# A four-layer kernel on one core: new token orders for the first convolution, moved product buffers, moved spectrum stores, and the last block's products in rows 1, 3, 5, 7

## The chip, the core and the metric

The kernel runs on one core of a Trainium2 chip. The metric is the device time of one execution in microseconds. A core has a matrix engine (PE; PEld is its weight load), a vector engine (DVE), a scalar engine (ACT), a general engine (POOL), and SP, whose queue issues nearly all DMAs here. Each engine runs its own instructions in order, and engines wait for each other through semaphores. Matmuls write PSUM, and ACT or DVE must copy ("evacuate") the result to SBUF.

## The reference

Four layers over x of shape 2048 x 512: local attention, long convolution, and both again with the same weights. Every layer works on a layer norm of x and adds its result to x.

```
def _A_ref(x, wqkv, wo):                 # 32 heads of 16
    q, k, v = split(x @ wqkv)
    idx = pos[:, None] - 2 * arange(8)   # 8 keys, every second position back
    attn = softmax(where(idx >= 0, q . k[idx] / 4, -1e9))
    return (attn . v[idx]) @ wo
def _B_ref(u, ...):                      # per channel
    K = real(sum_n Cc * exp(dt * A * l) * dt * Bc)
    return irfft(rfft(u, 2L) * rfft(K, 2L))[:L] + u * Dskip
x = x + _A_ref(ln(x)); x = x + _B_ref(ln(x))
x = x + _A_ref(ln(x)); x = x + _B_ref(ln(x))
```

## The kernel before

**Stages.** `k_gen` computes the convolution kernel K in tables (tiles A_t and A_t2 in two table pools, power table pow_t, B_t) and, beside it, the first layer's norm, keys and queries. At its end the first three products of the first attention are formed in tiles A_pr, which lie in the first table pool. Then come attention 0 (`LayerA.core`), convolution 0 (`FftB`, tag 0), attention 1 and convolution 1. All engines but POOL follow an order written out by hand.

**Attention** (`core`, line 307). Queries and keys are worked in 4 blocks (q) of 512 positions and 4 feature tiles (ft). `mult(q, ft)` (289) is one DVE instruction that multiplies a query tile with 8 shifted key tiles into a product tile of the pool `self.prp` (two buffers, 8 KB per partition each). `lsum` (298) sums the products over each head by 32 matmuls into the logits L. `mx` (360), `sub_exp` (366), `recip` (376) and `norm_p` (389) are the softmax. The loop at line 465 does blocks 0 to 2, with the value projections `v_proj` (346) and query projections between. The last value projections start a DMA that copies v one partition on (354, 355); without it no row but the first two can be worked.

The value phase is the loop at line 492 over 16 rows. `pv_mult` (397) is a DVE instruction of the same size (attention times values), `pv_sum` (405) sums it by 32 matmuls, `out_proj` (416) projects the row before and adds x. In between stand the products and the sums of block 3, its query projections and its softmax (max in row 8, reciprocal in row 10, normalisation in row 11):

```
q_proj(3, 0)
q_proj(3, 1)
...
if n in (1, 2, 4, 6):
    mult(3, n // 2)
...
if n in (2, 4):
    q_proj(3, n // 2 + 1)
```

**Convolution** (`FftB`, line 694). It has two groups of 256 channels. Its order is a string of tokens; the last letter says which engine evacuates (A: ACT, D: DVE).

- `K` and `U` (`f1`, 735): first transform of the convolution kernel and of the input, 16 tokens each, 8 for each group.
- `k` (`k_f2`, 754) and `u` (`u_f2`, 797): second transform; it needs all eight first ones of its group. u is always evacuated by ACT.
- `m` (`u_mult`, 786): the product of both spectra, two DVE instructions. Besides the spectrum tile kn it needs a copy ks with partitions exchanged pairwise, which two DMAs make (`kf_load`, 772).
- `y` (`i1`, 805): first inverse transform. `z` (`i2`, 821): second inverse transform and addition to x, with 8 matmuls for D and 12 for A.

All these share four PSUM tiles, so a token's matmuls wait until the fourth token before it is evacuated. Spectrum tiles come from a list `free`, taken from the front; `m` puts both tiles back at the end. `pump` (767) starts the exchange DMAs, at most `ahead` (4) spectra past the multiply. `k_f2` also stores the spectrum to kf_dram, from which convolution 1 reads it. The list `late` holds the last norm pieces of attention 0 (rows 8 to 15), one of which is done after each K token from the second on; U needs them all.

`ORDER0` covers convolution 0 up to half of the y tokens. `ORDERF` has the rest and, between, the front of attention 1: half statistics h, aggregation a, root p, norm n, transposes T with their evacuations E, and key and query projections P and Q.

Of the kernel before, what the change touches and what calls it, by code (L numbers as in the profile page):

```python
# [14 lines left out]
F32 = mybir.dt.float32  # L15
BF16 = mybir.dt.bfloat16
# [4 lines left out]
P = 128  # L21
S = 2048
# [15 lines left out]
NG = 2  # L38
DQG = 64
EC = 16  # L40
NEC = 128 // EC
# [6 lines left out]
zktkKkUEETkeUUktKTkkUkKTUUeKkkpkxpKUxkpUEUxUKkqUxUUUUpqoUkpoxKXUQxoUkpkKXZpxXxpxZZ  # L48
"""
ORDER0 = """  # L50
KA KD KA KD KA KA KD KA KD KA KD kA KD KA KA kD kA kD kA UA KD UA UA UD UA kD UA
UA UD KA UA kD u kD m u u u kA m UA m UD UA u kA m kD u UA u m UA m
UD m UA kA u kD kD u kA u m m kA m u u yD yA m u u m u m yA u yA
yA m m yA m yA yD
"""
ORDERF = """
yA yA yA yA yA yA z00D yA h00 yA z01D h01 z10A z11A h10 a0 p0 h11
n0 z12A z02A a1 z03A h12 S T0 h02 p1 E00A n1 E01A a2 z13A P00 h13 Q00
h03 T1 E10A p2 E11D P01 a3 P02 P03 P10 p3 P11 n2 n3 P12 T2 E20D E21A
P13 T3 E30A P20 P21 x1 P22 P23 E31D  # L60
"""
ORDER1 = """
UD UA UA UD UA UA UD UA UD UA UD u UD u m UA u u m UA m u u UA m UD m
# [52 lines left out]
def rstd_act(nc, pool, var):  # L116
    rstd = pool.tile(list(var.shape), F32, name="ln_rstd")
    nc.scalar.activation(rstd[:], var, ACT.Ln, bias=EPS)
    nc.scalar.activation(rstd[:], rstd[:], ACT.Exp, scale=-0.5)
    return rstd  # L120
# [42 lines left out]
class LayerA:  # L163
# [143 lines left out]
    def core(self, x_sb, u, lnp, ev=None, nprod=0):  # L307

        tc, nc, lnst, l = self.tc, self.nc, self.lnst, self.layer
# [11 lines left out]

        with ExitStack() as c2:
            big = c2.enter_context(tc.tile_pool(name=f"a{l}_big", bufs=1, reuse_waits="tile"))
            self.prp = c2.enter_context(tc.tile_pool(name=f"a{l}_prod", bufs=2, reuse_waits="tile"))
            v = big.tile([P, NA + 14, D], BF16, name="v_ext")
            if self.wv is None:
                self.load_wv(big)
# [1 line left out]
            if l:  # L329
                self.load_wo(big)  # L330
            wk = c2.enter_context(tc.tile_pool(name=f"a{l}_wk", bufs=2, reuse_waits="tile"))
            pavp = c2.enter_context(tc.tile_pool(name=f"a{l}_pav", bufs=2, reuse_waits="tile"))
            ps_q = c2.enter_context(tc.tile_pool(name=f"a{l}_ps_q", bufs=2, space=PSUM))
            ps_o = c2.enter_context(tc.tile_pool(name=f"a{l}_ps_o", bufs=2, space=PSUM))
# [60 lines left out]
            pvs, oTs, lns = {}, {}, {}  # L395
# [35 lines left out]
            def x_stats(a):  # L431
                row_stats(nc, lnst, x_sb[:, a, :], a, "dve")

            def u_begin(a0, a1, eng, rs="pool"):
                lns[a0] = ln_begin(nc, lnp, lnst, a0, a1, eng, rs)

            def u_end(a0):
                lns[a0] = ln_end(nc, lnp, lns[a0])

            def u_apply(a0, rows, eng=None):  # L440
                rstd, nb = lns[a0]
                for a in rows:
                    ln_apply(nc, u[:, :, a, :], x_sb[:, a, :].rearrange("p (q r) -> p q r", r=4), rstd, nb, a - a0,
                             eng or ("dve" if a % 2 else "act"))
# [42 lines left out]
            proj(100)  # L487
            linit(3)
            q_proj(3, 0)
            q_proj(3, 1)  # L490
            rows = [0, 2, 1, *range(3, NA)]
            for n in range(16):
                pv_mult(rows[n])
                if n in (0, 8):
                    mx(2 + n // 8)
                if n in (2, 10):
                    recip(2 + n // 8)
                if n in (4, 11):
                    norm_p(2 + n // 8)
                if n in (1, 2, 4, 6):  # L500
                    mult(3, n // 2)
                if n in (7, 11, 15):
                    u_begin(n - 7, n - 3, "act", "act" if n > 7 else "pool")
                if n in (8, 12):
                    u_end(n - 8)
                if n in (9, 10, 13, 14):
                    b0 = 0 if n < 11 else 4
                    r0 = b0 + (0 if n in (9, 13) else 2)
                    u_apply(b0, range(r0, r0 + 2))
                if n == 15:  # L510
# [12 lines left out]
                if n > 0:  # L523
                    out_proj(rows[n - 1])
                if n in (1, 2, 4, 6):
                    lsum(3, n // 2)
                event(("o", n))
            if l == 0:
                out_proj(15)
                return [lambda: [u_end(8), u_apply(8, range(8, 12), "pool")], lambda: x_stats(14), lambda: x_stats(15),  # L530
                        lambda: u_begin(12, 16, "dve", "act"), lambda: [u_end(12), u_apply(12, range(12, 16), "pool")]]
            u_begin(12, 15, "dve", "act")
            out_proj(15)
            pw = pq_tile()
# [159 lines left out]
class FftB:  # L694
# [566 lines left out]
def kernel(  # L1261
# [16 lines left out]
    nc = tc.nc  # L1278
# [18 lines left out]
    u = xnT[:].rearrange("p t (b r) -> p (t b) r", r=64).rearrange("p q (a r) -> p q a r", r=4)  # L1297
# [38 lines left out]
    with tc.tile_pool(name="ctmp_g2", bufs=1) as g2tmp, tc.manual_schedule(engines=MAN):  # L1336
# [9 lines left out]
    late.append(C["masks"])  # L1346
    krctx2.close()
    la.close_logits()

# [3 lines left out]
    fb.ahead = 4  # L1353
    fb.open_mid()
    with tc.manual_schedule(engines=MAN):
        fb.run(ORDER0, u, k=kp, late=late)
    fb.c_mid.close()
    la.close()
    la = LayerA(tc, nc, consts, lnst, A_wqkv, A_wo, 1, xnT, 1)
# [95 lines left out]
```

## Time and profile before

| What | us |
|---|---|
| median of 8 runs | 431.95 (430.49 to 433.6) |
| the profiled execution, its own time | 433.6 |
| its span, first to last instruction | 431.8 |
| stage: convolution kernel, keys and queries of layer 1 | 0 to about 112 |
| stage: attention 0, logits, then value rows | 112 to 141, 141 to 199.5 |
| stage: convolution 0 | 199.5 to 264.8 |
| stage: front and logits of attention 1 | 264.8 to 322 |
| stage: value rows of attention 1 | 322 to 378 |
| stage: convolution 1 | 380 to 431.8 |

Times inside the span are counted from its start. A bracket at the end of a timeline line is the idle time of the engine just before the instruction, and what ended it. In a group such as "x32" the first time is the start of the first. The costliest waits of PE, ACT and DVE that concern the stages above, from the table of waits, are these: PE's weight load for pav 8.3 us in 12 waits, DVE's cast for PE 7.3 us in 8, DVE's addition to x for PE 7.5 us in 5.

### The profile page before, as it was taken

How to read it: one execution, taken by the hardware profiler on the slowest of the kernel's cores; microseconds unless marked ns; L12 is line 12 of the kernel's file. 1: busy time of each engine (PE TensorE's matmuls, PEld its weight loads, DVE VectorE, ACT ScalarE, POOL GpSimd, SP SyncE). 2: the span in 40 equal slices, each digit the busy share in tenths (PEclk: the TensorE clock that was granted, in tenths of full speed). 3: DMA queues.
4: the chain of work that ended last, by engine and by line, in shares of the span. 5: the costliest groups of instructions: out<-in, count | busy, mean ns of one | idle time of the engine just before them, and what ended most of it. 6: DMA issues, size and time to landing. Idle time of an engine off the chain costs nothing.

```text
span 431.8 us, 12729 instructions
## 1 busy us (share of the span) xinstructions
PE 352.8 (82%) x5502; PEld 264.2 (61%) x5502; DVE 391.9 (91%) x534; ACT 325.8 (75%) x557; POOL 39.1 (9%) x46
## 2 busy tenths in 40 slices
PE   3000259899999989999888999999998999997894
PEld 2000127667655668676877897555566778776794
DVE  8999999999899999995899959879999999889874
ACT  6999999986355488986899998855556469689961
POOL 3000300000692000002200000000000020000000
PEclk9999999999999999999899999999999899999999
DMA  8930832141116742742355670810141085125415
GB/s 221 384 101 12 85 73 70 32 76 48 29 37 186 241 124 89 265 200 101 110 212 216 252 197 24 260 60 2 32 112 30 2 318 188 51 83 168 128 34 164
DMA packets 62466, 54.16 MB, mean 125 GB/s; under 512 B 33893, under 2 KB 50890, under 8 KB 61130
## 3 DMA queue, kind: packets, MB, share of 16 engines
q1 hardware_dynamic: 62266, 53.22, 40.2%
q8 instruction: 43, 0.70, 0.7%
q10 hardware_dynamic: 144, 0.13, 0.1%
q14 instruction: 13, 0.11, 0.1%
HBM read 30.28 MB, written 13.24 MB: 101 GB/s over the span
## 4 chain that ended last, share of the span: by engine, by line
PE 51%; ACT 12%; DVE 12%; DMA 5%; issue 3%; SPq 2%; ACTq 0%; DVEq 0%
PE po L410 9%; PE pk L1150 5%; DVE prod L295 5%; PE pq L349 4%; PE pq L422 4%; ACT a1s L733 4%; PE pp L1088 4%; PE L L302 3%; PE pp L242 3%; DVE pav L402 3%; ACT ub L803 3%; PE pq L185 3%; DMA v_ext<-v_ext 3%; PE pb L816 3%; PE pb L817 2%
## 5 line engine op out<-in xcount | busy, mean ns | idle before, releaser
L402 DVE TENSOR_TENSOR pav<-attn,v_ext 128x4096 bf16<-128x4096 bf16 x32 | 72.8, 2284 | 0.7 <-PE po L410 0.2
L295 DVE TENSOR_TENSOR prod<-qT,kT_ext 128x4096 bf16<-128x4096 bf16 x29 | 66.1, 2298 | 2.2 <-PE L L302 2.1
L410 PEld LDWEIGHTS <-pav 128*128 128x128 bf16 x1024 | 59.2, 98 | 12.2 <-DVE pav L402 8.3
L410 PE MATMUL po<-ident,pav 128*128 128x128 bf16 x1024 | 63.1, 220 | 4.1 <-DVE pav L402 4.0
L1078 PE MATMUL pt<-ident,x_blk 128*128 128x128 bf16 x64 | 6.3, 241 | 43.4 <-ACT x_blk L158 43.4
L990 DVE TENSOR_TENSOR A_t<-A_t,pow_t 128x1024 bf16<-128x1024 bf16 (+4 forms) x46 | 38.3, 872 | 0.2
L351 ACT CAST v_ext<-pq 128x512 bf16<-128x512 f32 x32 | 18.7, 586 | 21.1 <-PE pq L349 19.9
L803 ACT CAST ub<-pb 128x1024 bf16<-128x1024 f32 x32 | 33.0, 1089 | 1.4 <-DVE t L791 1.3
L422 PE MATMUL pq<-wop,oT 128*128 128x512 bf16 x128 | 33.7, 387 | 0.0
L302 PEld LDWEIGHTS <-prod 128*128 128x128 bf16 x928 | 26.8, 96 | 10.3 <-DVE prod L295 5.4
L1078 PEld LDWEIGHTS <-x_blk 128*128 128x128 bf16 x64 | 4.8, 107 | 45.8 <-ACT x_blk L158 44.4
L751 PE MATMUL pb<-a1s,w_sb 128*128 128x64 bf16 x768 | 27.6, 194 | 5.8 <-ACT ub L803 3.3
L816 PE MATMUL pb<-Wp,t 128*128 128x128 bf16 x256 | 30.1, 219 | 1.8 <-ACT ub L803 1.4
L1088 PE MATMUL pp<-xnT,kT_ext 128*128 128x512 bf16 x96 | 26.2, 400 | 6.1 <-ACT qT L1093 3.2
L733 ACT CAST a1s<-pb 128x1024 bf16<-128x1024 f32 x30 | 29.4, 1076 | 1.8 <-PE pb L744 1.7
L349 PE MATMUL pq<-wv,xnT 128*128 128x512 bf16 x128 | 30.7, 379 | 0.0
L413 ACT CAST oT<-po 128x512 bf16<-128x512 f32 x32 | 18.5, 579 | 15.6 <-PE po L410 15.6
L751 PEld LDWEIGHTS <-w_sb 128*128 128x128 bf16 x768 | 25.1, 98 | 8.3 <-issue 7.1
L817 PE MATMUL pb<-WpJ,t 128*128 128x128 bf16 x256 | 30.1, 219 | 0.0
L302 PE MATMUL L<-ind,prod 128*128 128x8 bf16 x928 | 27.5, 166 | 1.8 <-DVE prod L295 1.6
L733 DVE CAST a1s<-pb 128x1024 bf16<-128x1024 f32 x18 | 21.7, 1222 | 7.5 <-PE pb L744 7.3
L817 PEld LDWEIGHTS <-t 128*128 128x128 bf16 x256 | 25.0, 98 | 2.6 <-issue 1.5
(226 smaller groups left out, 855.5 us busy)
## 6 DMA issues: line engine op xcount, KB each, us to landing
w_sb<-w_dram SPq DMA_DIRECT2D x8, 1024.0 KB, 7.8
w_dram<-w_zero SPq DMA_DIRECT2D x1, 4096.0 KB, 14.5
kf_ring<-kf_dram SPq DMA_DIRECT2D x13, 256.0 KB, 3.6
kf_ring<-kf_dram SPq DMA_DIRECT2D x26, 128.0 KB, 3.6
v_ext<-v_ext SPq DMA_DIRECT2D x4, 784.0 KB, 6.1
x_blk<-in_A_x_dram SPq DMA_DIRECT2D x4, 512.0 KB, 4.1
kT_ext<-in_A_wqkv_dram SPq DMA_DIRECT2D x4, 512.0 KB, 9.8
x_sb<-in_A_x_dram SPq DMA_DIRECT2D x4, 512.0 KB, 5.1
```

Of the source, the lines that this page charges most:

```text
L295: nc.vector.tensor_tensor(pr, self.qT[q][:, ft].unsqueeze(1).to_broadcast([P, W, 4, P]), kap, ALU.mult)
L302: self.nc.tensor.matmul(L[:, al, w, ft * 8:(ft + 1) * 8], lhsT=pr[:, w, al, :], rhs=self.c["ind8"][:], start=(ft == 0 and w == 0 and al % ...
L349: nc.tensor.matmul(pp[:], lhsT=xnT[:, dt, a * P:(a + 1) * P], rhs=wv[:, dt, :], start=(dt == 0), stop=(dt == NDT - 1))
L402: nc.vector.tensor_tensor(pv[:], attn[:, n % 4].unsqueeze(2).to_broadcast([P, W, DH, H]), vap, ALU.mult)
L410: nc.tensor.matmul(po[:, ft, :], lhsT=pvf[:, w, ft * P:(ft + 1) * P], rhs=ident[:], start=(w == 0 and ft == 0), stop=(w == W - 1), skip_gr ...
L422: nc.tensor.matmul(pw[:], lhsT=oT[:, ftp, :], rhs=self.wo[:, ftp, :], start=False, stop=(ftp == NDT - 1))
L733: (self.nc.scalar.copy if eng == "act" else self.nc.vector.tensor_copy)(dst, src)
L751: nc.tensor.matmul(p2[:, j, :], lhsT=self.w2[:, ec * EC + j, :], rhs=a1s[:, ec * EC + j, :], start=True, stop=True)
L803: nc.scalar.copy(ub[:], p2)
L816: nc.tensor.matmul(p3[:, j, :], lhsT=t1[:, dql, :], rhs=wp_r, start=True, stop=False)
L817: nc.tensor.matmul(p3[:, j, :], lhsT=t2[:, dql, :], rhs=wpj_r, start=False, stop=True)
L1088: nc.tensor.matmul(pps[kind, b, ft][:], lhsT=la.wqk[:, dt, c:c + P], rhs=la.xnT[:, dt, b * 512:(b + 1) * 512], start=(dt == 0), stop=(dt = ...
```

## The change

1. The product pool is opened after the pool wk instead of before it; in attention 0 a 2 KB tile named gap is put between.
2. In the value phase block 3's products are formed, and summed, in rows 1, 3, 5, 7 instead of 1, 2, 4, 6. Of its query projections only the first is left before the rows; the other three are in rows 1, 3, 5.
3. `ORDER0` and `ORDERF` are replaced. ORDER0 now ends after three y tokens instead of eight, and ORDERF has thirteen. ACT evacuates 10 k, 10 U, 7 K and 13 y (before 8, 12, 9 and 14); DVE 6, 5, 9 and 3 (before 8, 4, 7, 2). One z is on DVE instead of two, four E instead of three. The new string has 15 U tokens where the old one has 16: the first transform of the last 32 channels of group 1 is left out, and the second transform reads what that part of its tile holds.
4. The late pieces are named and ordered by a string; aggregation (g) and root (r) are two pieces instead of one, so there are seven with the masks instead of six. The masks' instructions are POOL's, and in the profile they run at 44 us.
5. The store of the spectrum moves from behind `k_f2` to behind the multiply of the same spectrum. `pump` may now also start an exchange, in convolution 0, whenever more tiles are free than spectra are still to come.

```diff
 ORDER0 = """
-KA KD KA KD KA KA KD KA KD KA KD kA KD KA KA kD kA kD kA UA KD UA UA UD UA kD UA
-UA UD KA UA kD u kD m u u u kA m UA m UD UA u kA m kD u UA u m UA m
-UD m UA kA u kD kD u kA u m m kA m u u yD yA m u u m u m yA u yA
-yA m m yA m yA yD
+KD KA KA KD KA KA KD KA KD KA KD kA kA KD kA KD UA UD UA UD UA kD UA UD UA KD
+kA kD u kD kA u UA m KD m u u UA UA UA m UD u m KA UD u m u kA kD m kA UA
+kD u kA m kA kD u m u kA m m u u yD yA u m yA u m m m u u m m
 """
+LATE0 = "a s t g r b m"
 ORDERF = """
-yA yA yA yA yA yA z00D yA h00 yA z01D h01 z10A z11A h10 a0 p0 h11
-n0 z12A z02A a1 z03A h12 S T0 h02 p1 E00A n1 E01A a2 z13A P00 h13 Q00
-h03 T1 E10A p2 E11D P01 a3 P02 P03 P10 p3 P11 n2 n3 P12 T2 E20D E21A
-P13 T3 E30A P20 P21 x1 P22 P23 E31D
+yA yA yA yA yA yA yD yA yA yA z01D yD yA yA z00A z10A z11A h01 h00 h10 a0 z12A
+p0 h11 z02A n0 a1 z03A h02 S T0 p1 E01D n1 E00A h12 a2 z13A P02 P01 h03 T1
+E10A Q00 E11D p2 P03 P00 n2 h13 P10 P12 a3 T2 E21D E20A p3 n3 P11 P13 P23 P21
+T3 E31D x1 E30A P20 P22
 """
...
-            self.prp = c2.enter_context(tc.tile_pool(name=f"a{l}_prod", bufs=2, reuse_waits="tile"))
...
             wk = c2.enter_context(tc.tile_pool(name=f"a{l}_wk", bufs=2, reuse_waits="tile"))
+            if l == 0:
+                wk.tile([P, 1024], BF16, name="gap", bufs=1)
+            self.prp = c2.enter_context(tc.tile_pool(name=f"a{l}_prod", bufs=2, reuse_waits="tile"))
...
+            def u_aggr(a0, a1):
+                ag = lnp.tile([P, a1 - a0, 2], F32, name="ln_ag")
+                for a in range(a0, a1):
+                    nc.vector.bn_aggr(ag[:, a - a0, :], lnst["bn"][:, a, 0, :])
+                lns[a0] = ag
+            def u_rstd(a0):
+                ag = lns[a0]
+                lns[a0] = rstd_act(nc, lnp, ag[:, :, 1]), ag[:, :, 0], -1.0
...
-            q_proj(3, 1)
...
-                if n in (1, 2, 4, 6):
+                if n in (1, 3, 5, 7):
                     mult(3, n // 2)
...
-                if n in (2, 4):
+                if n in (1, 3, 5):
                     q_proj(3, n // 2 + 1)
...
         self.nk += 1
         self.pump()
-        self.nc.sync.dma_start(self.kf_dram[g, ec].rearrange("p r q e -> (p r) (q e)"), kf.rearrange("p q e -> p (q e)"))
...
+    def room(self):
+        return self.tag == 0 and len(self.free) > NG * NEC - self.nk
     def pump(self):
-        while self.nkf < min(self.nk, self.nm + self.ahead):
+        while self.nkf < self.nk and (self.nkf < self.nm + self.ahead or self.room()):
             self.kf_load(self.nkf)
...
         self.nm += 1
         if self.tag == 0:
+            self.nc.sync.dma_start(self.kf_dram[g, ec].rearrange("p r q e -> (p r) (q e)"), kn.rearrange("p q e -> p (q e)"))
             self.free += [kn, ks]
```

More of the change, by code (lines that the diff above doesn't have):

```diff
@@ L50 @@
 ORDER0 = """
-KA KD KA KD KA KA KD KA KD KA KD kA KD KA KA kD kA kD kA UA KD UA UA UD UA kD UA
-UA UD KA UA kD u kD m u u u kA m UA m UD UA u kA m kD u UA u m UA m
-UD m UA kA u kD kD u kA u m m kA m u u yD yA m u u m u m yA u yA
-yA m m yA m yA yD
+KD KA KA KD KA KA KD KA KD KA KD kA kA KD kA KD UA UD UA UD UA kD UA UD UA KD
+kA kD u kD kA u UA m KD m u u UD UA UA UA m UD u m KA UD u m u kA kD m kA UA
+kD u kA m kA kD u m u kA m m u u yD yA u m yA u m m m u u m m
 """
+LATE0 = "a s t g r b m"
 ORDERF = """
-yA yA yA yA yA yA z00D yA h00 yA z01D h01 z10A z11A h10 a0 p0 h11
-n0 z12A z02A a1 z03A h12 S T0 h02 p1 E00A n1 E01A a2 z13A P00 h13 Q00
-h03 T1 E10A p2 E11D P01 a3 P02 P03 P10 p3 P11 n2 n3 P12 T2 E20D E21A
-P13 T3 E30A P20 P21 x1 P22 P23 E31D
+yA yA yA yA yA yA yD yA yA yA z01D yD yA yA z00A z10A z11A h01 h00 h10 a0 z12A
+p0 h11 z02A n0 a1 z03A h02 S T0 p1 E01D n1 E00A h12 a2 z13A P02 P01 h03 T1
+E10A Q00 E11D p2 P03 P00 n2 h13 P10 P12 a3 T2 E21D E20A p3 n3 P11 P13 P23 P21
+T3 E31D x1 E30A P20 P22
 """
@@ L524, in core @@
                     out_proj(rows[n - 1])
-                if n in (1, 2, 4, 6):
+                if n in (1, 3, 5, 7):
                     lsum(3, n // 2)
@@ L529, in core @@
                 out_proj(15)
-                return [lambda: [u_end(8), u_apply(8, range(8, 12), "pool")], lambda: x_stats(14), lambda: x_stats(15),
-                        lambda: u_begin(12, 16, "dve", "act"), lambda: [u_end(12), u_apply(12, range(12, 16), "pool")]]
+                return {"a": lambda: [u_end(8), u_apply(8, range(8, 12), "pool")], "s": lambda: x_stats(14), "t": lambda: x_stats(15),
+                        "g": lambda: u_aggr(12, 16), "r": lambda: u_rstd(12),
+                        "b": lambda: [u_end(12), u_apply(12, range(12, 16), "pool")]}
             u_begin(12, 15, "dve", "act")
@@ L1345 @@
         late = la.core(x_sb, u, lnp, ev, 3)
-    late.append(C["masks"])
+    late["m"] = C["masks"]
     krctx2.close()
@@ L1355 @@
     with tc.manual_schedule(engines=MAN):
-        fb.run(ORDER0, u, k=kp, late=late)
+        late["."] = lambda: None
+        fb.run(ORDER0, u, k=kp, late=[late[c] for c in LATE0.split()])
     fb.c_mid.close()
```

## The prediction

> **What bounds the kernel now.** I read the page's engine shares first, then the busy time by stage (windows), then the timelines of single engines at the places the diff touches, and last the DMA queue.
>
> ```profile
> PE 352.8 (82%) x5502; PEld 264.2 (61%) x5502; DVE 391.9 (91%) x534; ACT 325.8 (75%) x557; POOL 39.1 (9%) x46
> 141.00:178.00 37.00, 34.64 (x515) 26.26 (x513) 36.59 (x30) 28.17 (x56) 1.02 (x1) 1.00 0.54 154
> 199.50:264.80 65.30, 58.48 (x1357) 54.70 (x1357) 54.92 (x87) 59.83 (x68) 6.37 (x9) 0.97 0.51 176
> 268.30:320.50 52.20, 52.15 (x616) 30.19 (x615) 45.73 (x63) 32.42 (x58) 0.00 (x0) 1.00 0.29 89
> 340.00:378.00 38.00, 37.91 (x517) 29.76 (x516) 35.04 (x42) 26.82 (x66) 2.89 (x1) 1.00 0.45 162
> ```
>
> The columns after the length are busy PE, PEld, DVE, ACT and POOL. DVE's 91% is an average over stages with different limits. In the first attention's value phase (141 to 178 us) DVE is full. In the first convolution (199.5 to 264.8) nobody is: ACT 59.8 and PE 58.5 of 65.3. In the second attention's front and logits, and again from 340 to 378, PE is full. So the same edit is worth something in one layer and nothing in another.
>
> Four places show waits that the diff could touch (timelines of DVE, PE and ACT):
>
> ```profile
> 112.15 0.44 DVE L255 COPY kT_ext<-kT_ext 128x508 bf16<-128x508 bf16 x1
> 114.66 4.49 DVE L295 TENSOR_TENSOR prod<-qT,kT_ext 128x4096 bf16<-128x4096 bf16 x2 [2.08 <-PE L L302]
> ```
> ```profile
> 113.68 0.94 PE L302 MATMUL L<-ind,A_pr 128*128 128x8 bf16 x32
> ...
> 117.01 0.95 PE L302 MATMUL L<-ind,prod 128*128 128x8 bf16 x32 [0.64 <-DVE prod L295]
> ```
> ```profile
> 204.54 0.20 ACT L118 ACTIVATE ln_rstd<-ln_ag 128x4 f32<-128x4 f32 x1 [1.50 <-DVE ln_ag L128]
> ...
> 213.78 7.47 ACT L733 CAST a1s<-pb 128x1024 bf16<-128x1024 f32 x8
> ```
> ```profile
> 255.53 1.23 DVE L836 TENSOR_TENSOR x_sb<-pb,x_sb 128x1024 bf16<-128x1024 f32 x1 [5.01 <-PE pb L833]
> ```
> ```profile
> 334.62 2.54 PE L410 MATMUL po<-ident,pav 128*128 128x128 bf16 x32 [1.25 <-DVE pav L402]
> ```
> ```profile
> kf_dram<-kn SPq DMA_DIRECT2D x7, 256.0 KB, 3.4
> DMA to landing us min/median/max: 2.3/3.2/4.6
> ```
>
> The first pair is the important one: DVE stops for 2.08 us until PE has read A_pr. The product doesn't need A_pr; only its memory does. The last fence is the landing of the spectrum stores (line 761), which the change moves.
>
> **What the Trainium skill says.** Perfetto Trace Analysis, Optimization Strategy: a kernel can have several regimes; look for gaps on the engine that limits each one and for the semaphore behind them. The trace agrees (windows above). DMA: Bandwidth & Descriptors, Two DMAs through the same engine are not ordered: only the completion semaphore orders, so a buffer that a store still reads can't be rewritten before the store has landed; here 2.3 to 4.6 us. SBUF — State Buffer, Who interferes with whom: a DVE instruction with two SBUF inputs contends with a GpSimd one that reads SBUF. The trace agrees in part: at 129.19 us, beside POOL, a product takes 2.70 us against 2.28, but the two from 114.66 are not slowed. TensorE: Matmul & The Clock Gate, What's actually happening: the PE clock halves for windows of 3.4 us after slack. The trace has such windows from 206.1 and from 335.81, each 3.41 us; the second follows the 1.25 us gap above.
>
> **The change part by part.**
>
> *Product buffers (first attention).* Sizes per partition: the products begin 74 KB or so above the constants (residual 16.8, small tiles 0.3, spectrum 16, g2 scratch 8, v and wo 34), i.e. 75 KB to 91 KB. The tables of the kernel generation lie at 64 to 80 (A_t) and 80 to 88 (A_t2), and hold A_pr. That is the overlap behind the 2.08 us. Behind the wk pool (11 KB) and the gap (2 KB) the products begin at 88 KB, past A_t2, over the second table pair, whose last reader (pk, line 1150) ends at 111.1, before DVE is ready at 112.6. So the stall goes. What is late next: the max (line 363) of this block needs the row sums on PE. PE: 4 value projections and two row sums from 111.96 end at 116.2; row sum 0.8 and mask 0.5 bring 117.6, where DVE would stand at 117.05. So DVE keeps 2.08 - 0.55 = 1.5 us. PE's waits for prod (0.79, 0.58, 0.24, 0.36 and 0.30 up to 141) add to 2.2, so PE can follow. DVE is full from there to 183.6, hence **-1.5** at 199.5. Bounds: -2.1 (no wait at the max) and -0.8 (POOL beside DVE costs 0.4 a product twice). The copy of v by DMA (issue 141.15, landing 147.9, needed 148.87) is moved with the projection that starts it and keeps its 1 us.
>
> *Products in rows 1, 3, 5, 7, projections in 1, 3, 5.* Nothing is added; four products of 2.2 us and three projections of 0.86 move. First attention: DVE-bound, the sum before row 8 is the same, 0. The row sum of the last product now comes in row 7; row 8's max needs it at 173.65 and PE has it at 172.95. Second attention: PE idles 0.17 + 0.15 + 1.25 = 1.57 before row 4. Now the projection no longer stands before row 2, which waits for the v copy (326.88): PE idles 1.03 there, and 0.1 later: -0.5. But the max of block 3 now waits for PE: 352.7 instead of 351.36; 13.4 us later (chain to pav of row 12) DVE comes about 0.5 late for PE. I take **-0.2**; bounds -0.5 and +0.3. The half-clock window costs 3.41/2 = 1.7 us; the profiled execution (433.6, span 431.8 and 1.8 around it) pays it, and 433.6 - 1.7 is the median 431.95. So I sum against the median and count no gain there.
>
> *ORDER0, ORDERF, late list.* Counting tokens with the measured spacing (ACT 0.905, DVE cast 1.14, multiply pair 1.2): ACT up to the last i2 58.8 before, 57.0 after; DVE 45.5 and 46.6. One U token fewer (0.44 PE, 0.9 ACT) is in it. ACT ran without a gap from 213.8 to 258. More to the point is the prefix: at the last multiply ACT had 45.3 and DVE 42.0; now 40.7 and 43.1. Splitting aggregation and root saves ACT the 1.50 wait. POOL's second apply (3.0 us) starts at 205.6 instead of 205.28; the first U comes at 209.6, later. Walking: first u evacuated at 217.8, DVE then full to the last multiply at 246.15 (before 249.0). PE is without a gap from y3: 13 y at 0.92, one i2 at 0.88, six at 1.31 = 20.7 from 241.9, i.e. 262.65 against 264.84: **-2.2**. DVE's start of the tail moves from 255.5 to 252.2, which covers one more cast, one more transpose copy (0.6) and a 1.4 wait for z00's ACT copy; the last norm ends 0.9 earlier, so PE's projections stay gapless.
>
> *Moved store.* 16 stores at 0.55 issue each go from behind the spectrum to behind its multiply; the SP queue issues the same 26 us. Behind a waiting swap stand all later swaps and stores. New wait: swap 4 takes kn0, free at multiply 0 (220.15); store 1 is issued by 221.9; swap 6 takes kn1 and waits for it, 221.9 + L; two issues 1.1 and store 3's 0.6; kD9 takes kn3, free at 223.6 + 2L, and is due on DVE at 228.4. Stall = 2L - 4.8, with 0.35 slack. With L = 3.2 (median): 1.6, net **+1.25**. Bounds: L = 2.3 gives 0, L = 4.6 gives +4.05. Queued behind kD9 on DVE: the multiplies 5 to 15, and for them all of y8 to z13. The later group-1 swaps are issued at once (free buffers outnumber what is left), which takes the 0.26 wait of multiply 12; already in the walk.
>
> Sum: -1.5 - 0.2 - 2.2 + 1.25 = -2.65; 431.95 - 2.65 = **429.3** (the profiled kind of execution: 433.6 - 2.65 = 430.95, or 429.25 without the half clock).
>
> **The rivals.**
> All of it (20%): stores land within 2.6, the max doesn't wait: -2.1 - 0.2 - 2.2 = -4.5, 427.45. For: 2.2 to 2.5 is what swaps and kf_nat stores take. Against: the SP queue is near full there.
> Only the memory wait (18%): the convolution's balance brings nothing, as DVE is now filled to 100% and any lag of 1.1 reaches y8: -1.5, 430.45. For: DVE's idle was its slack. Against: ACT had 2.7 idle too.
> It doesn't do what it says (7%): the moved buffers still meet live memory (the gap is 2 KB, my sum of sizes is good to some 0.3 KB), and the 2.08 stays: -1.2, 430.75.
> Slower (13%): the store-before-reuse chain at kD9. The total is 2L - 9.05; it decides from L = 4.5 on, the upper end of what stores showed (4.6). With L = 5.2, +1.35, 433.3. For: v_ext copies took 6.1. Against: stores no longer alternate with the swaps early on.
>
> **How the numbers follow.** Forecast 42% at 429.3 (428.2 to 430.4 alone), the others as given. 0.3% is 1.3 us, what a measurement of this kernel can tell from no change: faster is under 430.65, slower over 433.25. Faster: 42 + 20 + 10 of the 18 = 72; slower: 11 of the slow case's 13; the rest 17. Range: 426.8 to 431.6 leaves out the slow case and a little of the fastest.
>
> **What would show it.** The 2.08 before the first prod gone and the value phase's end 1.5 earlier; z03's last matmul some 1 us earlier relative to the convolution's start; a DVE wait of 1 to 2 us before the tenth k cast put down to a DMA; in the second attention PE idle near row 2 and no 1.25. Wrong if the wait before prod stays, if the k casts wait 4 us or more, or if PE has gaps between y3 and z13.

## The result and the profile after

| What | before | after |
|---|---|---|
| median, us | 432.01 (32 runs) | 428.43 (11 runs) |
| lowest to highest, us | 430.49 to 435.29 | 428.15 to 428.70 |
| profiled execution, its own time, us | 433.6 | 428.58 |
| its span, us | 431.8 | 426.8 |

The ratio is 0.9913, with a 95% interval of 0.9896 to 0.9929: 3.6 us less. The forecast was 429.3 with a range of 426.8 to 431.6. The spread (highest less lowest) fell too, from 4.8 us to 0.55.

One correction comes first. The copy of the new `ORDER0` above lacks a token: its second line reads `... m KD m u u UD UA UA UA m UD ...`. So there are sixteen U tokens, ACT evacuates ten and DVE six of them, and nothing is left out of the computation. Point 3 of the change and the "one U token fewer" of the prediction are my misreading.

The busy shares of the changed kernel (page), and busy time by stage (windows: length, then PE, PEld, DVE, ACT, POOL, granted clock, DMA share, GB/s). The stretches follow the same work as those shown of before:

```profile
PE 354.2 (83%) x5506; PEld 264.3 (62%) x5506; DVE 394.7 (92%) x537; ACT 323.2 (76%) x554; POOL 43.9 (10%) x46
```
```profile
141.00:178.00 37.00, 35.87 (x505) 27.57 (x503) 36.66 (x29) 28.22 (x56) 1.02 (x1) 0.95 0.53 149
198.90:264.10 65.20, 61.29 (x1389) 56.03 (x1388) 58.65 (x99) 60.74 (x70) 6.37 (x9) 1.00 0.52 176
264.10:315.20 51.10, 51.05 (x585) 29.36 (x583) 45.69 (x69) 31.53 (x57) 0.00 (x0) 1.00 0.30 91
337.00:373.00 36.00, 35.53 (x480) 27.16 (x479) 34.21 (x42) 24.98 (x61) 2.89 (x1) 1.00 0.48 170
```

The first convolution takes 65.2 us instead of some 67, and DVE is busier in it (58.65 us in 65.2 against 54.92 in 65.3): from 207.1 until the last multiply ends at 245.66 its timeline shows no idle time. The stretch of attention 1 is still PE's. The 0.95 of the first stretch is a half-clock window from 141.76. It costs nothing there, where DVE is the limit: the value rows of attention 0 take 58.28 us, as in a_noroom and a_store2, runs told of below, which have no such window (58.28 and 58.29). The next table has each stage from its first instruction to the next stage's; the runs beside the two kernels are told of below:

| us | before | after | p_only | r_only | c_only | c_oldstore | a_g2act |
|---|---|---|---|---|---|---|---|
| logits of attention 0, from the last key copy | 28.98 | 28.34 | 28.58 | 29.22 | 28.98 | 28.98 | 26.67 |
| value rows of attention 0 | 58.35 | 58.28 | 58.34 | 58.26 | 58.34 | 58.34 | 58.29 |
| convolution 0 | 67.83 | 65.21 | 67.04 | 67.38 | 65.20 | 66.95 | 65.21 |
| front and logits of attention 1 | 51.53 | 51.07 | 51.53 | 51.53 | 51.07 | 51.06 | 51.07 |
| value rows of attention 1 | 61.64 | 60.23 | 59.82 | 61.04 | 59.82 | 59.94 | 60.15 |
| convolution 1 | 51.33 | 51.40 | 51.30 | 51.31 | 51.44 | 51.18 | 51.07 |

The profiled execution of before is 1.6 us above its median; it has half-clock windows from 206.1 and from 335.81. The second costs some 1.8 us (value rows of 61.64 us, against 59.82 in p_only with the same rows and no window). So the difference of the profiled executions, 5.0 us, is larger than the 3.6 of the medians.

DVE at the first products, after. The wait of 2.08 us is gone, and the max now waits 0.17 for PE:

```profile
112.79 4.80 DVE L295 TENSOR_TENSOR prod<-qT,kT_ext 128x4096 bf16<-128x4096 bf16 x2
117.76 1.22 DVE L365 TENSOR_REDUCE mx<-L 128x128 bf16<-128x1024 f32 x1 [0.17 <-PE L L285]
...
136.03 0.82 DVE L381 TENSOR_TENSOR s<-ex 128x512 bf16<-128x512 bf16 x1
136.89 0.67 DVE L383 TENSOR_TENSOR s<-s 128x256 bf16<-128x256 bf16 x1
```

POOL's timeline at that place, in the kernel before and then after:

```profile
112.43 1.38 POOL L684 TENSOR_SCALAR g_i<-g_i,aux 128x512 int32<-128x512 int32 x2
```

```profile
112.54 5.53 POOL L696 TENSOR_SCALAR g_i<-g_i,aux 128x512 int32<-128x512 int32 x2
...
132.15 5.26 POOL L696 TENSOR_SCALAR k_perm<-k_perm,aux 128x512 int32<-128x512 int32 x2
```

The second column is the duration. POOL's first two multiply-adds took 1.38 us while DVE stood still, and 5.53 us beside DVE's product. All of POOL's work ends 5 us later, at 137.4, and so the sums from 136.03 on take 0.82 and 0.67 us; in the kernel before, the same two sums stood behind POOL's end and took 0.41 and 0.29.

DVE's timeline around the tenth k cast (227.81), after:

```profile
227.21 0.68 DVE L805 TENSOR_TENSOR t<-ub,w_sb 128x1024 bf16<-128x1024 bf16 x1
227.81 1.22 DVE L745 CAST kn<-pb 128x1024 bf16<-128x1024 f32 x1
228.95 0.68 DVE L805 TENSOR_TENSOR t<-ub,kf_sb 128x1024 bf16<-128x1024 bf16 x1
```

SP's queue ahead of it (line 791 is an exchange, 808 a store), after:

```profile
217.98 1.10 SPq L791 DMA_DIRECT2D w_sb<-kn  x2
219.13 0.58 SPq L808 DMA_DIRECT2D kf_dram<-w_sb  x1
...
222.67 1.10 SPq L791 DMA_DIRECT2D w_sb<-kf_sb  x2
223.82 0.58 SPq L808 DMA_DIRECT2D kf_dram<-kn  x1
```

No bracket stands behind the cast: nothing waited. Store 1 left at 219.13 and store 3 at 223.82, some 2.3 us before the forecast had them (0.6 of it because the whole convolution began earlier). By the profile store 3 landed 2.3 us after it left, at 226.12, which is 1.7 us before the cast.

PE's timeline in row 2 of attention 1, after:

```profile
323.72 0.94 PE L302 MATMUL L<-ind,prod 128*128 128x8 bf16 x32
325.59 1.96 PE L412 MATMUL po<-ident,pav 128*128 128x128 bf16 x32 [0.93 <-DVE pav L404]
```

ACT's timeline at the late root, after:

```profile
203.63 0.24 ACT L118 ACTIVATE ln_rstd<-ln_ag 128x4 f32<-128x4 f32 x1
```

PE's gap of 1.25 us in row 3 has become 0.93 us in row 2, and ACT's wait of 1.50 us before the root is gone.

### The profile page after: what moved, and what is told of

It reads as the page before. It is cut to its first block, busy times and chain, and to the rows that moved or that the text cites. A ratio compares the mean times of both kernels' runs of the same rounds, so it can differ in the third digit from the quotient of the medians.

```text
span 426.8 us, 12737 instructions
## 1 busy us (share of the span) xinstructions
PE 354.2 (83%) x5506; PEld 264.3 (62%) x5506; DVE 394.7 (92%) x537; ACT 323.2 (76%) x554; POOL 43.9 (10%) x46
## 4 chain that ended last, share of the span: by engine, by line
PE 47%; DVE 22%; ACT 7%; DMA 4%; issue 3%; SPq 2%; DVEq 0%; ACTq 0%
PE po L412 8%; PE pk L1165 5%; DVE pav L404 5%; DVE prod L295 4%; PE pq L351 4%; DVE t L805 4%; PE pp L1103 4%; PE pq L424 4%; PE L L302 3%; DVE a1s L745 3%; PE pp L242 3%; PE pq L185 2%; PE pb L831 2%; PE pb L832 2%; DMA v_ext<-v_ext 1%
## 5 line engine op out<-in xcount | busy, mean ns | idle before, releaser
L424 PE MATMUL pq<-wop,oT 128*128 128x512 bf16 x128 | 32.8, 379 | 0.0
L1103 PE MATMUL pp<-xnT,kT_ext 128*128 128x512 bf16 x96 | 27.9, 421 | 4.4 <-ACT xnT L1096 1.7
L745 DVE CAST a1s<-pb 128x1024 bf16<-128x1024 f32 x22 | 26.1, 1218 | 4.9 <-PE pb L756 4.8
L745 ACT CAST a1s<-pb 128x1024 bf16<-128x1024 f32 x26 | 25.6, 1043 | 2.0 <-PE pb L756 2.0
```

The source lines that it names most:

```text
L424: nc.tensor.matmul(pw[:], lhsT=oT[:, ftp, :], rhs=self.wo[:, ftp, :], start=False, stop=(ftp == NDT - 1))
L745: (self.nc.scalar.copy if eng == "act" else self.nc.vector.tensor_copy)(dst, src)
L1103: nc.tensor.matmul(pps[kind, b, ft][:], lhsT=la.wqk[:, dt, c:c + P], rhs=la.xnT[:, dt, b * 512:(b + 1) * 512], start=(dt == 0), stop=(dt = ...
```

## Experiments

Names that begin with p, r, c and b are the kernel before with one part of the change or one edit; those that begin with a are the changed kernel with one part undone or altered.

### The parts alone

Each of the three takes a part of the change; c_only is the whole change without these two parts (orders, late list, stores, pump):

```diff
 # p_only
-            self.prp = c2.enter_context(tc.tile_pool(name=f"a{l}_prod", ...
...
+            if l == 0:
+                wk.tile([P, 1024], BF16, name="gap", bufs=1)
+            self.prp = c2.enter_context(tc.tile_pool(name=f"a{l}_prod", ...
 # r_only
-            q_proj(3, 1)
...
-                if n in (1, 2, 4, 6):
+                if n in (1, 3, 5, 7):
...
-                if n in (2, 4):
+                if n in (1, 3, 5):
```

The runs were made in three sets, each with runs of the kernel before among them; its medians were 432.64 (the first four), 432.44 (a_oldstore, a_noroom, a_unsplit, a_g2act) and 433.07 us (the last four).

> The kernel before with the moved product pool and its gap alone. Theory (POOL's index work, which used to run in DVE's 2.08 us of idle time, now runs beside DVE and takes part of the gain back): no wait before the first prod, POOL's first two tensor_scalars take about 5.5 us in sum instead of 1.4, POOL is done 5 us later, the first value row starts 0.5 us earlier on DVE and convolution 0 about 0.6 earlier; time about 431.4. Rival (as forecast, the max waits 0.55 for PE and the rest is kept): 1.5 us earlier in both places, time 430.5. Rival (the gain is lost again before the convolution): 432.0.

> The kernel before with rows 1, 3, 5, 7 and the moved query projections alone. Theory (the new order takes away the 1.25 us PE gap in row 3 of attention 1 and with it a half-clock window that most executions of the kernel before pay): no half-clock window between 325 and 345 us, the value phase of attention 1 is 1.4 us shorter, time about 430.5, and the spread of its runs is clearly below the 4.8 us of before. Rival (as forecast, the waits only move): 0.2 us, time 431.8, spread as before, or a half-clock window behind the new gap of about 1 us in row 2.

> The kernel before with the new orders, the split late list, the moved stores and the wider pump, without the pool and the rows. Theory: the whole convolution gains what the trace of the changed kernel shows, 2.7 us from its first K matmul to the last matmul of the last z, no DMA wait before DVE's tenth k cast; time about 429.3. Rival (as forecast, a store wait of 1.6 us at that cast): 1 us, time 431.0. If the half-clock window near 206 us is in most executions of before, its absence is part of the gain, and the time is 429.0 or less.

| run | median, us | ratio to before | 95% interval | in us of 432 |
|---|---|---|---|---|
| p_only | 431.59 | 0.9970 | 0.9957 to 0.9982 | -1.3 |
| r_only | 432.39 | 0.9998 | 0.9981 to 1.0015 | -0.1 |
| c_only | 429.44 | 0.9942 | 0.9919 to 0.9964 | -2.5 |

The three add up to -3.9, and the whole is -3.8 of 432: within these intervals there is no sign that the three parts lean on each other. In p_only POOL's first pair takes 5.53 us, as expected, and the logits of attention 0 are 0.4 us shorter; the key copy that begins the stage took 0.68 us in that execution and 0.44 in before, and without it the gain is 0.64, as in the changed kernel. The ratio says 0.8 us at the least; what else p_only gained, its one profile doesn't show.

In r_only the wait has only moved. DVE's timeline in row 2 of attention 1:

```profile
324.02 2.28 DVE L295 TENSOR_TENSOR prod<-qT,kT_ext 128x4096 bf16<-128x4096 bf16 x1
327.38 2.29 DVE L402 TENSOR_TENSOR pav<-attn,v_ext 128x4096 bf16<-128x4096 bf16 x1 [1.08 <-DMA v_ext<-v_ext]
```

PE's timeline there, in the same run:

```profile
327.04 0.94 PE L302 MATMUL L<-ind,prod 128*128 128x8 bf16 x32
329.73 1.96 PE L410 MATMUL po<-ident,pav 128*128 128x128 bf16 x32 [1.75 <-DVE pav L402]
```

The copy of v, which row 2 needs, lands 1.08 us too late, and PE stands for 1.75 us behind it, more than the 1.40 (0.15 and 1.25) that the new rows took away. There is no half-clock window after it, though. The times of r_only spread over 4.1 us (430.43 to 434.56), nearly as those of before. In c_only DVE waits for no DMA in the convolution, as expected.

### What of the convolution does it

```diff
 # c_oldstore: c_only, and a_oldstore: the changed kernel, with
-        while self.nkf < self.nk and (self.nkf < self.nm + self.ahead or self.room()):
+        while self.nkf < min(self.nk, self.nm + self.ahead):
...
 # and the store behind the second transform's self.pump() again
 # a_noroom: the changed kernel with the first two lines alone
```

> As the run c_only, but with the stores behind the second transform and the pump as before. Theory (stores lie under other work in either place, and nothing on DVE waits for them): within 0.3 us of c_only, 429.3. Rival (as forecast, the moved store costs 1.25 us): faster than c_only by about 1.2. Rival (the stores stand before the exchanges in SP's queue and make the multiplies late; the move is what lets the new order work): slower than c_only by 0.5 to 2, with DVE multiplies that wait for a DMA.

> The changed kernel with the stores back behind the second transform and the pump as before. Theory (the orders alone bring next to nothing, since with the stores ahead of the exchanges in SP's queue the multiplies of the second group wait for exchanges; the moved stores and the wider pump are what the gain hangs on): DVE multiplies from the eleventh on wait 1 to 3 us for a DMA, time 430.4 to 430.9, spread of the runs over 2 us. Rival (that was particular to the run c_oldstore, by way of a different start of the convolution): within 0.5 us of the changed kernel, 428.4 to 428.9.

> The changed kernel with the stores moved but the pump's limit of four exchanges as before. Theory (the stores' place is what counts, the exchanges' own limit is not): no DVE wait for a DMA, 428.4 to 428.7. Rival (the earlier start of the last exchanges is what counts): waits of 1 us or more before multiplies from the eleventh on, 429.5 to 430.5.

| run | median, us | lowest to highest | ratio to before | 95% interval |
|---|---|---|---|---|
| c_oldstore | 432.24 | 430.30 to 434.36 | 0.9994 | 0.9977 to 1.0011 |
| a_oldstore | 431.22 | 430.38 to 433.94 | 0.9990 | 0.9975 to 1.0005 |
| a_noroom | 432.08 | 430.07 to 433.17 | 0.9974 | 0.9955 to 0.9993 |

This was the surprise. With the stores where they had been, the new orders are worth nothing that can be measured. With the stores moved but the pump's limit kept, most of the gain is still missing, against the expectation that the stores' place alone counts. DVE's timeline near the last multiplies of a_noroom:

```profile
243.37 0.70 DVE L805 TENSOR_TENSOR t<-ub,kf_nat 128x1024 bf16<-128x1024 bf16 x1
245.97 0.69 DVE L805 TENSOR_TENSOR t<-ub,kf_sb 128x1024 bf16<-128x1024 bf16 x1 [1.90 <-DMA kf_sb<-kf_nat]
```

SP's queue in a_noroom, with the exchange that it waits for (kf_sb<-kf_nat):

```profile
236.83 2.28 SPq L791 DMA_DIRECT2D kn<-kf_nat  x2
239.15 0.58 SPq L808 DMA_DIRECT2D kf_dram<-kn  x1
239.83 1.10 SPq L791 DMA_DIRECT2D w_sb<-kf_nat  x2
240.98 0.58 SPq L808 DMA_DIRECT2D kf_dram<-kf_nat  x1
241.66 1.11 SPq L791 DMA_DIRECT2D kf_sb<-kf_nat  x2
```

And the same stretch of SP's queue in the changed kernel:

```profile
231.43 5.24 SPq L791 DMA_DIRECT2D kf_nat<-kf_nat  x6
236.71 0.58 SPq L808 DMA_DIRECT2D kf_dram<-kf_sb  x1
237.40 1.90 SPq L791 DMA_DIRECT2D kf_nat<-kf_nat  x2
239.39 1.18 SPq L791 DMA_DIRECT2D w_sb<-kn  x2
```

SP issues back to back in both stretches; a pair of exchange DMAs mostly takes 1.1 to 1.2 us to issue (some take up to 2.3), a store 0.58. In a_noroom each exchange of the second group has a store ahead of it, and that of the fifteenth spectrum leaves at 241.66. It holds up the multiply until 245.97, a wait of 1.90 us. In the changed kernel six exchange DMAs go first, that one leaves at 239.39, and nothing waits. In a_oldstore the last multiply waits 1.50 us for its exchange. In c_oldstore DVE's waits are 1.13 and 0.35 us (its timeline):

```profile
241.86 1.29 DVE L805 TENSOR_TENSOR t<-ub,kf_nat 128x1024 bf16<-128x1024 bf16 x2 [1.13 <-DMA kf_nat<-kf_nat]
...
247.21 0.69 DVE L805 TENSOR_TENSOR t<-ub,w_sb 128x1024 bf16<-128x1024 bf16 x1 [0.35 <-DMA w_sb<-kf_nat]
```

These waits, 1.90 us in a_noroom, 1.50 in a_oldstore and 1.48 in c_oldstore, are most of what their convolutions have more than 65.2 us (2.1, 2.4 and 1.7). The profiled execution of c_oldstore is its fastest, at 430.30; its median is 2 us above that. So the gain hangs on the order of SP's queue, and the wider pump is needed. Two things were not run: the wider pump with the stores in their old place, so that the move of the stores is needed too is not shown; and both edits with the old orders.

The times of these three runs spread over 3 to 4 us, as those of before do, and those of the changed kernel don't. The profiles show one source of it. With the old orders too DVE waits for an exchange, that of the twelfth spectrum. First b_g2act, then r_only (DVE's timeline):

```profile
240.95 1.29 DVE L795 TENSOR_TENSOR t<-ub,kn 128x1024 bf16<-128x1024 bf16 x2 [0.21 <-DMA kn<-w_sb]
```
```profile
243.17 1.29 DVE L790 TENSOR_TENSOR t<-ub,kn 128x1024 bf16<-128x1024 bf16 x2 [1.33 <-DMA kn<-w_sb]
```

The same wait is 0.99 us in p_only. The three convolutions take 66.27, 67.38 and 67.04 us (b_g2act, r_only, p_only); less the wait each is 66.05 or 66.06. So one and the same order is late by a different amount each time. By this sum, an estimate, the new order gains 0.85 us of the convolution plus whatever the old one waited. The changed kernel isn't proof against it: in an execution of a_unrows, which has the same convolution, the second half of the last exchange left at 242.01 and landed 4.0 us later; in the changed kernel's profile it left at 241.81 and landed 2.1 us later. DVE's timeline in a_unrows:

```profile
246.10 0.69 DVE L806 TENSOR_TENSOR t<-ub,w_sb 128x1024 bf16<-128x1024 bf16 x1 [0.93 <-DMA w_sb<-kf_sb]
```

Its convolution takes 66.23 us instead of 65.21. Half-clock windows go with the late executions as well: in c_oldstore the ten with a mean granted clock of 0.998 or more took 430.30 to 432.46 us, the eight at 0.991 or less 432.44 to 434.36. How much of the spread is due to each stays open.

### The store chain that the forecast priced

```diff
 # a_kd9early
-... u u UD UA UA UA m ... u kA kD m kA UA
+... u u UA UA UA m ... u kA kD UD m kA UA
 # a_store2
-            self.nc.sync.dma_start(<all 128 rows>)
+            for h in range(2):
+                self.nc.sync.dma_start(<64 rows of it>)
```

> The changed kernel with the tenth U token on DVE moved from behind u3 to behind the tenth k, so that DVE comes to that k cast 1.14 us earlier, at about 226.7 instead of 227.8, while the work is the same. Theory (the chain of stores and exchanges that the forecast priced is there, and the changed kernel just misses it: store 3 leaves at 223.8 and lands 2.3 to 3.9 us later, 226.1 to 227.7): DVE waits up to 1 us for a DMA before the tenth k cast, time 428.4 to 429.0. Rival (no such chain): no wait there, same time within 0.3.

> The changed kernel with each spectrum stored in two halves, so that SP issues 16 DMAs of about 0.55 us more. Theory (SP's queue has little slack there; what decides is how early the exchanges leave): the tenth k cast waits 0.3 to 1 us for a store, the exchanges of the second group leave 2 us or more later and multiplies wait for them, time 429.5 to 431. Rival (SP has slack enough): 428.4 to 428.7.

a_kd9early: 429.13 us, ratio 0.9911 (0.9881 to 0.9941). Its cast came 0.45 us earlier, not 1.14, and what it waited 0.31 us for was PE:

```profile
227.36 1.23 DVE L745 CAST kn<-pb 128x1024 bf16<-128x1024 f32 x1 [0.31 <-PE pb L763]
```

Store 3 left at 223.59 and landed 2.5 us later, at 226.09. So this run shows no wait for a store, and can't refute one, since it brings the cast only part of the way to the landing. a_store2 is clear: 432.41 us, ratio 0.9997 (0.9976 to 1.0018), the whole gain gone. DVE's timeline in it:

```profile
227.21 0.69 DVE L805 TENSOR_TENSOR t<-ub,w_sb 128x1024 bf16<-128x1024 bf16 x1
229.58 1.23 DVE L745 CAST kn<-pb 128x1024 bf16<-128x1024 f32 x1 [1.67 <-DMA kf_dram<-kn]
...
248.91 0.69 DVE L805 TENSOR_TENSOR t<-ub,w_sb 128x1024 bf16<-128x1024 bf16 x1 [1.98 <-DMA w_sb<-kf_sb]
```

The tenth k cast waits 1.67 us for a store, and the last multiply 1.98 us for an exchange. The chain of the "slower" rival exists, at the place the forecast gave. The second half of store 3 leaves there at 226.47 and lands 2.9 us later, at 229.39, just before the cast; in the changed kernel store 3 lands at 226.12, with 1.7 us to spare. The last exchange leaves at 244.98 instead of 241.30, and lands too late for the last multiply. The profiled execution is 1.3 us above the median of its run and has a half-clock window from 250.54, behind PE's wait for that multiply.

### The late pieces

```diff
-LATE0 = "a s t g r b m"
+LATE0 = "a s t g . b m"    # with root in g
```

> The changed kernel with aggregation and root of rows 12 to 15 as one late piece again, in the place of the aggregation. Theory (the split takes a wait off ACT that stalls PE's first K tokens): ACT waits about 1.5 us at ln_rstd, PE has gaps of about 1 us among the K tokens, the convolution is 0.5 to 1 us longer, 429.0 to 429.4. Rival (DVE, which is full from there on, hides it): 428.4.

429.01 us, ratio 0.9926 (0.9902 to 0.9950); the convolution takes 65.77 us instead of 65.21. ACT's timeline at the root:

```profile
203.63 0.21 ACT L118 ACTIVATE ln_rstd<-ln_ag 128x4 f32<-128x4 f32 x1 [0.64 <-DVE ln_ag L442]
```

ACT waits 0.64 us there, less than expected, but its later casts come late for PE, which stands 1.17 us before the tenth K token (0.10 in the changed kernel). The split is worth some 0.6 us.

### The rows within the changed kernel

In a_unrows the lines of the rows and projections are those of before:

```diff
-            q_proj(3, 0)
+            q_proj(3, 0)
+            q_proj(3, 1)
...
-                if n in (1, 3, 5, 7):
+                if n in (1, 2, 4, 6):
...
-                if n in (1, 3, 5):
+                if n in (2, 4):
```

> The changed kernel with block 3's products back in rows 1, 2, 4, 6. Theory (the rows bring nothing on their own, as in the run r_only; PE's gap only moves from row 3 to row 2): within 0.4 us of the changed kernel, 428.1 to 428.8. Rival (together with the rest the rows are worth something, and the gap of row 3 brings back the half-clock window of attention 1): 429 to 430, with more spread.

428.73 us, ratio 0.9914 (0.9887 to 0.9942): the median is the same. But two of its six times are 430.29 and 431.13, while the eleven of the changed kernel end at 428.70. The profiled one is that of 431.13. PE's timeline in row 3:

```profile
329.87 0.95 PE L302 MATMUL L<-ind,prod 128*128 128x8 bf16 x32
332.07 2.72 PE L412 MATMUL po<-ident,pav 128*128 128x128 bf16 x32 [1.25 <-DVE pav L404]
```

The windows view of the stretch after it (the third number from the end is the granted clock):

```profile
333.07:336.48 3.41, 3.19 (x22) 2.25 (x21) 3.41 (x3) 0.58 (x1) 0.00 (x0) 0.50 0.00 0
```

PE runs at half clock (0.50) from 333.07, and the value rows take 61.64 us, as in before, 1.4 us more than in the changed kernel. The window is only half of why this execution is late: 1.0 us is the late exchange shown above, which has nothing to do with the rows. c_only has the same gap of 1.25 us, no window after it, and 59.82 (PE's timeline):

```profile
331.22 1.96 PE L410 MATMUL po<-ident,pav 128*128 128x128 bf16 x32 [1.25 <-DVE pav L402]
```

Of the six profiled executions with the old rows two have the window; of the eight with the new rows none has. That points to the rows as insurance against it, at a price of up to 0.4 us (1.2 in r_only) where none falls; so few profiles don't settle it. For it speaks the mean granted clock, 0.986 and 0.991 in the two late executions of a_unrows and 0.993 to 0.995 in the other four; against it, that r_only, which has the new rows too, spreads over 4.1 us.

### Taking POOL out

```diff
 # a_g2act: the changed kernel, and b_g2act: the kernel before, with
-            nc.gpsimd.tensor_scalar(g, g, p21, bias, ALU.mult, ALU.add)
...
+    def scales(h):
+        for k, bias in enumerate((16384.0, 32768.0)):
+            g = gi[h][:, k * 4 * P:(k + 1) * 4 * P]
+            nc.scalar.activation(g, g, ACT.Identity, scale=p21, bias=bias)
...
+              ("m", 1, 0): [G(gm, 0)], ("m", 1, 1): [G(gm, 1)], ("m", 1, 2): [G(gm, 2)], ("m", 1, 3): [G(gm, 3)],
```

> The changed kernel with the eight index instructions (multiply and add) that POOL does beside DVE in attention 0 done by ACT instead, two in front of each product of block 1. Theory (POOL's use of SBUF beside DVE costs DVE what it lost: two slow small sums twice, a longer product, 0.8 us after the wait was gone, as much again in the kernel before): all sums at 0.42 and 0.29 us, products at 2.28, the first value row on DVE 1.5 us or more earlier than in the changed kernel, time 427.0 to 427.6. Rival (DVE's lost time there is made up anyway, or ACT's 4 us delay the evacuations PE needs): 428.4 or more.

> The kernel before with the eight index instructions on ACT instead of POOL. Theory (they slow DVE in the kernel before as well, by 0.4 in the first sums, 0.4 in the next, 0.4 in one product; the 2.08 us wait before the first prod stays): the first value row 1.2 us earlier, ratio about 0.997. Rival (their first two fell into DVE's idle time and the others cost nothing that is not made up): ratio 1.0.

| run | median, us | ratio to before | 95% interval |
|---|---|---|---|
| a_g2act | 426.87 | 0.9874 | 0.9848 to 0.9901 |
| b_g2act | 431.85 | 0.9964 | 0.9947 to 0.9982 |

a_g2act beats both kernels: its four times (426.54 to 427.01) all lie below the fastest of the changed kernel. DVE's timeline in it:

```profile
112.92 4.50 DVE L295 TENSOR_TENSOR prod<-qT,kT_ext 128x4096 bf16<-128x4096 bf16 x2
117.88 1.23 DVE L365 TENSOR_REDUCE mx<-L 128x128 bf16<-128x1024 f32 x1 [0.47 <-PE L L285]
...
135.27 0.42 DVE L381 TENSOR_TENSOR s<-ex 128x512 bf16<-128x512 bf16 x1
135.73 0.29 DVE L383 TENSOR_TENSOR s<-s 128x256 bf16<-128x256 bf16 x1
```

ACT's timeline, with the first two multiply-adds:

```profile
117.13 1.33 ACT L700 ACTIVATE g_i<-g_i,aux 128x512 int32<-128x512 int32 x2
```

All sums are at 0.42 and 0.29 us, and two multiply-adds take ACT 1.33 us. The logits of attention 0 take 26.67 us instead of 28.34. Now the max waits 0.47 us for PE, near the 0.55 that the forecast had. In b_g2act the 2.07 us wait stays and the logits take 27.78 us instead of 28.98. So with POOL out of the way the moved buffers are worth 27.78 - 26.67 = 1.1 us there, with POOL beside DVE 0.64 (0.4 in p_only, with the longer copy).

## Why the prediction was right or wrong

**Product buffers, -1.5: right in kind, too large in the stage.** The wait went and the max became late, as forecast (0.17 us, since POOL had already slowed the products: 4.80 us for two instead of 4.49). At the max 1.44 us of the 2.08 were still there (it starts 5.49 us after the key copy instead of 6.93), about what the sum had. What failed is the step after it, that DVE would keep them: POOL's work had used DVE's idle time and now runs on for 5 us, and the two sums from 136.03 on lose 0.79 us to it, so that the stage kept 0.64. The lower bound (-0.8) had POOL for its reason, but in the products; the value taken should have been near it, because the evidence was in the profile of before. The two products "from 114.66" that "are not slowed" don't speak against it: the sums at 124.61 and 125.47 of that timeline took 0.83 and 0.66 us, the same sums at 137.34 and 137.79, after POOL's end, only 0.41 and 0.29. The time of p_only (-1.3, interval -1.9 to -0.8) agrees with the forecast better than the stage does.

**Rows, -0.2: not told apart from nothing.** r_only gives -0.1 (-0.8 to +0.6), and in the stages the new rows cost a little where no half-clock window falls (59.88 to 61.04 us in eight profiles, against 59.82 to 60.02 in four with the old rows). The gap forecast for row 2 was 1.03 us; it measured 0.93 in the changed kernel and 1.75 in r_only. By r_only, leaving the half-clock window out of the sum made no difference to the median that can be measured.

**Orders and late list, -2.2, and moved store, +1.25: the sum of -0.95 was too small, and both terms were wrong.** Measured together: -2.5 (-3.5 to -1.6). In the stages it is 1.1 to 2.2 us of the convolution, which took 66.27 to 67.38 with the old orders in the three profiles without a half-clock window there (p_only, r_only, b_g2act), and 0.46 of the front of attention 1, for which the forecast had nothing. The wait of multiply 12, 0.26 in the profile that the forecast had, is 0.21 to 1.33 in those three.

The first failing step is the stall at the tenth k cast. The sum had store 3 landing at 223.6 + 2L = 230.0; it landed at 226.12. About half of the difference is L: the median of 3.2 was taken, and the two stores of this chain landed 2.3 us after they left, the sum's own lower bound, which gives no stall. The other half is the start: "swap 4 takes kn0, free at multiply 0 (220.15)", but it issued at 217.98. PE began the first U at 208.0 (the walk had 209.6), the first u was evacuated by 216.15 and not at 217.8, and the first of the multiply's two instructions frees the tile. The token that I misread doesn't change the outcome: it stands before that cast, so my walk brought DVE there a cast of 1.14 us too early against the chain; with it the formula would have given 0.5 us of stall and not 1.6.

The second is the sign. The forecast counted the moved store as a cost with a risk and the wider pump as a wait of 0.26 us taken away, "already in the walk". In fact the -2.2 depends on them: without both, the orders give -0.3 (c_oldstore, -1.0 to +0.5). The walk had moved the last multiplies forward by nearly 3 us and didn't ask whether SP, on which I had counted 26 us of issue, would have their exchanges there by then. With the old queue it doesn't.

That the total came within a microsecond is in part luck, because errors of both signs met. The stall of 1.25 us did not come and the 0.46 of the front was missing; on the other side the product term was 0.9 too large in its stage, and the 2.2 is the upper end of what the convolution shows. The main lever, the order of SP's queue, was in the sum with the wrong sign.

**PE gapless from y3 on:** right but for two places, 0.27 us before y3 and some 0.7 us at y8, which waits for the last multiply; the last matmul of z03 stands at 261.45 (forecast 262.65), 62.56 us from the convolution's start instead of 65.25. That is 2.7 us earlier, where the forecast's sign had some 1 us.

**The rivals.** "All of it" is nearest to the outcome on the convolution's side: its condition, stores that land within 2.6 us, held in the chain. It is wrong on the max, which does wait. "Only the memory wait" is refuted by c_only. "It doesn't do what it says" is refuted by the first product. The slower one is real as a mechanism, as a_store2 shows, and wasn't reached.

## What to carry to other kernels

When an order brings the consumers of a transfer forward, walk the issuing queue too: each DMA ahead of the one that is needed costs its issue time, and stores that nobody waits for belong behind the loads that somebody does. Start those loads as soon as a buffer is free: here moving the stores without that brought little. When a wait is taken away, look at which engine worked in it; here POOL's work had been free only because DVE stood still, and moving it to ACT, which had room, brought more in the stage (1.7 us) than removing the wait (0.64). Look at the spread of a kernel's times as well as its median: a change may cut off the late executions and leave the middle where it was.

## What the hardware showed that was not expected

- The Trainium skill, SBUF — State Buffer, Who interferes with whom, says that a DVE instruction with two SBUF inputs contends with a GpSimd one that reads SBUF, and that issue order decides who blocks. The runs agree on the first (no run tests the order), and give the sizes: two 128x512 int32 multiply-adds on POOL take 1.38 us alone and 4.7 to 5.6 beside DVE; DVE's 128x512 sum goes from 0.42 to 0.83 us and its 128x256 sum from 0.29 to 0.66, while a 128x4096 product loses at most 0.4 of 2.28. In proportion the short instructions pay most. The same section says that ACT never waits for others: two of the same multiply-adds take ACT 1.33 us, and DVE's sums beside them 0.42 and 0.29.
- The Trainium skill, TensorE: Matmul & The Clock Gate, What's actually happening, has PE go to half clock after an idle window of some 3.4 us, in free-running windows. The length agrees (3.41 us), and so does the chance in it: in a_unrows the window opened 1.0 us after the end of a 1.25 us gap, and after the same gap in c_only there was none. But PE was never idle for 3.4 us before it: in the 3.41 us ahead of the window of a_unrows it was busy for 2.02. So here the measurement decides: half clock can follow a gap of 1.25 us.
- The time that SP takes to issue is a cost where multiplies wait for exchanges: 16 more DMAs of about 0.6 us, one per store, made the last exchange leave 3.7 us later, and took back the whole gain (a_store2).
- The landing of one and the same exchange differs between executions: 2.1 us after it left in the changed kernel, 4.0 in a_unrows.
